# The first 300 pieces of a kernel that is written as a list of pieces, in another order

## The chip, the core and the metric

One Trainium2 chip, one core. The metric is device microseconds of one execution. The kernel before took 281.7, 282.6 and 284.32 us in three runs, median 282.6. One further execution was profiled. TensorE (PE) multiplies, VectorE (DVE), ScalarE (ACT) and GpSimd (POOL) work elementwise, SyncE (SP) issues the transfers. PE writes to PSUM, in four tiles here, called banks.

## The reference

Chunked attention feeds a gated causal convolution block. Batch 8, 8 heads, sequence 576, head width 64, model width 512.

```python
scores = scale * np.matmul(q_c, k_c.transpose(0, 1, 2, 4, 3))   # chunks of 64 tokens
scores = scores - np.max(scores, axis=-1, keepdims=True)
attn = np.exp(scores)
attn = attn / (np.sum(attn, axis=-1, keepdims=True) + 1e-09)
out = np.matmul(attn, v_c)                                      # becomes x, 8 x 576 x 512
...
gate_pre += conv_w[k][None, None, :] * xp[:, k:k + S, :]        # five taps
gate = 1.0 / (1.0 + np.exp(-gate_pre))
val = x @ w_val
return (gate * val @ w_out).astype(np.float32)
```

## The kernel before

The 4608 tokens are cut into nine groups of 512 (g = 0 to 8). In each group the eight heads stand as two pairs of tiles (p = 0, 1), and a pair can be worked on in two halves (b = 0, 1). The program is one list of short pieces, the string `ORDER` (line 19). The loop at line 634 runs through it and calls one small function for each piece. Every instruction goes through `run` (line 136, `tc.keep_in_program_order`), so each engine executes its own instructions in the order of the list, and all instructions carry line 137 in the profile. No scheduler changes it. Each engine is a queue of its own: a piece of PE that waits holds up every later piece of PE, and SP, POOL, DVE and ACT do likewise. SP keeps at most eight transfers in flight: each further one waits until the transfer eight places ahead of it has landed. `SLOTS` (line 85) gives each tile its buffer, each PSUM tile its bank, and each pair one of two probability tiles.

The pieces that matter here, with arguments group, pair, half:

- `lq`, `lk`, `lv`: load q, k, v of a pair, 512 KB, or 256 KB for a half. `lw n c`: load unit c of weight n (v for `w_val`, o for `w_out`), 512 KB. `lc`: load the convolution weights.
- `w1` to `w9`, `wa`, `wb`, `Q`, `wc`: the weights come as 64-bit floats and are made into a high and a low part of 32 bits (`v_hi`, `v_lo`). `Q` is three matmuls that sum parts on PE, with `wc` copying the sum out; `wa` and `wb` do that on POOL or DVE. `w5` is ACT, `w8` POOL, `w58` the two in one instruction on DVE. A D behind a name moves the piece to DVE, a G to POOL.
- `S`: scores, 16 small matmuls a half, which the trace shows as 32 rows. `mx`: maximum on DVE. `sb` then `ex`: subtract the maximum on DVE, exponential on ACT. In their place `mh`, `M`, `exM`: DVE splits the maximum into two parts (two instructions of 8 columns), PE subtracts them in the bank with four matmuls of 256 columns, ACT takes the exponential from the bank.
- `sm`: sum and reciprocal on DVE. `nm`: normalise on POOL. `T`: transposes on PE. `ec`: copy on ACT. `A`: probabilities times v on PE. `xr` (ACT) and `xd` (DVE): x as high and low part; `xc` keeps x for the convolution.
- `V g m c term`: one product of 512 columns for `val`. m is the output quarter, c the input quarter (c = 2 and 3 need pair 1, c = 0 and 1 pair 0), the term says which parts. Weight unit 3 holds c = 2, 3 with m = 2, 3; unit 2 c = 2, 3 with m = 0, 1; unit 1 c = 0, 1 with m = 2, 3; unit 0 the rest. `V 1 m c` without a term is three products.
- `k0`, `k`: taps of the convolution on ACT and DVE. `W n short`: matmuls on zeros that only keep PE active.

`HALVES` (line 632) makes pairs that have `xr` by halves keep their scores in a bank for each half, which holds for pair (0, 1). `LESS` (line 633) lists halves with an `M` piece; their score matmuls then accumulate. So a second `M` in the list is all that the program needs for the other half.

Of the kernel before, what the change touches and what calls it, by code (L numbers as in the profile page):

```python
# [22 lines left out]
T 0 1 0,ex 0 1 1,sb 0 0,ex 0 0,Q v 3,S 1 0 1,sm 0 1 1,sm 0 0,ec 0 1 0,wc v 3,wc v 2,S 1 0 0,lw v 0,w1G v 0,nm 0 1 1,w2 v 0,
mx 1 0,sb 1 0,T 0 1 1,ec 0 1 1,lv 0 1,A 0 1 0,xc 0 1 0,xr 0 1 0,xd 0 1 0,A 0 1 1,xr 0 1 1,xc 0 1 1,nm 0 0,T 0 0,ec 0 0,w3 v 0,
V 0 3 2 1,ex 1 0,V 0 2 2 2,V 0 1 3 1,w4 v 0,V 0 1 2 2,w9,V 0 1 2 1,w6 v 0,V 0 3 2 0,w7 v 0,w58 v 0,xd 0 1 1,lv 0 0,A 0 0,lw o 3,
V 0 1 2 0,V 0 2 3 1,V 0 0 2 2,w1G o 3,V 0 1 3 0,V 0 2 3 0,V 0 1 3 2,xr 0 0,V 0 2 3 2,xc 0 0,lw o 0,wa v 0,lk 1 1,V 0 0 2 1,
sm 1 0,lq 1 1,S 1 1 1,S 1 1 0,xd 0 0,V 0 0 0 0,nm 1 0,mx 1 1,wbD v 0,k0 0 2,V 0 3 3 2,k0 0 3,k0 0 1,ng 1 1,k 0 1 1,V 0 2 2 1,
V 0 3 1 1,w3 o 3,k0 0 0,k 0 0 1,T 1 0,V 0 0 3 2,V 0 2 0 2,w2 o 3,w4 o 3,V 0 1 1 1,V 0 2 1 2,lq 2 0,k 0 0 3,V 0 3 0 0,V 0 2 0 0,
ec 1 0,lv 1 0,w7 o 3,A 1 0,V 0 2 0 1,ea 1 1,k 0 2 1,V 0 3 1 2,k 0 3 2,w6 o 3,V 0 3 3 1,V 0 1 0 1,V 0 2 2 0,V 0 3 0 1,w58 o 3,
lv 1 1,k 0 0 2,V 0 2 1 1,V 0 3 3 0,rc 1 1,xr 1 0,xc 1 0,V 0 3 2 2,lk 2 0,V 0 0 1 0,V 0 0 1 2,V 0 3 1 0,V 0 2 1 0,V 0 3 0 2,  # L30
V 0 0 1 1,lw o 1,k 0 3 1,S 2 0 0,S 2 0 1,mx 2 0,vc 0 1,V 0 1 0 2,lq 2 1,w1G o 0,V 0 1 0 0,V 0 0 3 1,V 0 0 0 1,V 0 0 0 2,
V 0 1 1 0,lw o 2,lq 6 1,w5 o 0,xd 1 0,lq 8 1,lk 2 1,V 0 0 2 0,lk 3 0,lq 4 0,V 0 1 1 2,V 0 0 3 0,lv 3 1,nm 1 1,lq 3 1,lk 3 1,
lv 2 0,lk 4 0,vc 0 0,lq 3 0,w1G o 1,lv 2 1,w1G o 2,T 1 1,sb 2 0,V 1 2 0,ec 1 1,V 1 0 0,w3 o 1,k 0 2 2,ex 2 0,A 1 1,k 0 1 2,
w2 o 2,sm 2 0,S 2 1 0,xr 1 1,S 2 1 1,V 1 1 0,w5 o 2,xd 1 1,nm 2 0,w2 o 0,V 1 1 1,w2 o 1,V 1 0 1,mx 2 1,xc 1 1,V 1 3 2,ng 2 1,
k 0 3 3,V 1 0 3,ea 2 1,w3 o 2,V 1 0 2,k 0 0 4,V 1 1 2,k 0 1 3,T 2 0,w4 o 1,V 1 2 2,w7 o 1,k 0 2 3,V 1 3 3,k 0 1 4,V 1 3 0,
k 0 2 4,ec 2 0,V 1 3 1,w4 o 2,V 1 1 3,w3 o 0,k 0 3 4,S 3 0 0,sg 0 0,S 3 0 1,rc 2 1,w7 o 2,A 2 0,nm 2 1,mx 3 0,vc 1 0,V 1 2 3,
xr 2 0,sb 3 0,V 1 2 1,w8 o 2,sg 0 1,T 2 1,xd 2 0,vc 1 1,S 3 1 0,w4 o 0,S 3 1 1,ec 2 1,waD o 3,V 2 0 0,gs 0 0,xc 2 0,A 2 1,
w6 o 0,w7 o 0,V 2 2 0,gs 0 1,xr 2 1,V 2 0 1,lk 8 1,lq 5 1,w8 o 0,xd 2 1,V 2 1 0,V 2 2 1,ex 3 0,xcD 2 1,wa o 0,V 2 3 2,k0 1 0,
V 2 3 0,sm 3 0,wb o 0,gr 0 0,S 4 0 0,S 4 0 1,k0 1 2,mx 3 1,nm 3 0,V 2 2 2,gr 0 1,V 2 0 2,mx 4 0,k0 1 1,V 2 0 3,w6 o 2,hc 0 0,
ng 3 1,hc 1 0,sb 4 0,hc 0 1,V 2 2 3,wb o 3,ea 3 1,V 2 1 3,gdD 0 0,V 2 1 2,T 3 0,k 1 1 1,V 2 1 1,lv 4 0,lk 5 1,lk 7 0,lq 4 1,  # L40
lk 4 1,lv 3 0,lk 5 0,lv 8 0,waD o 2,V 2 3 1,wbD o 2,V 2 3 3,gdD 0 1,ec 3 0,S 4 1 0,S 4 1 1,rc 3 1,vc 2 0,k 1 1 2,A 3 0,ex 4 0,
nm 3 1,mx 4 1,P 0 2 0,w5 o 1,xcD 3 0,P 0 2 2,vc 2 1,P 0 3 2,w8 o 1,sb 4 1,w6 o 1,P 0 2 3,xr 3 0,T 3 1,wa o 1,sm 4 0,P 0 3 0,
ec 3 1,wb o 1,xd 3 0,S 5 1 0,ex 4 1,S 5 1 1,hc 2 1,A 3 1,nm 4 0,k0 3 0,sm 4 1,V 3 0 0,xr 3 1,P 0 3 3,mx 5 1,xc 3 1,nm 4 1,
P 0 2 1,k0 1 3,P 0 3 1,xd 3 1,k0 2 0,V 3 1 1,k0 2 2,k 1 0 1,V 3 0 1,oc 0 1,k 1 3 1,V 3 1 2,k 1 2 1,k0 3 1,T 4 0,k 1 1 3,V 3 2 0,
lv 4 1,ng 5 1,ec 4 0,k 1 0 2,V 3 2 3,k 1 3 2,k0 2 1,V 3 1 3,k 1 2 2,k0 2 3,V 3 3 0,k 1 3 3,ea 5 1,P 0 0 0,k 2 2 1,V 3 1 0,
k 2 0 1,V 3 3 3,k 1 2 3,V 3 2 2,k 2 2 2,V 3 0 2,k 1 1 4,P 0 1 0,k 1 0 3,P 0 1 3,k 1 2 4,k 1 0 4,P 0 0 1,k 2 3 1,P 0 1 1,sg 1 0,
k 1 3 4,V 3 0 3,lq 8 0,lk 6 0,lk 6 1,st 0 1,lq 7 0,lq 5 0,lk 8 0,lq 6 0,k 2 1 1,V 3 3 1,vc 3 0,k 2 3 2,P 0 0 3,sg 1 1,k 2 0 2,
T 4 1,gs 1 0,V 3 2 1,ec 4 1,V 3 3 2,rc 5 1,gr 1 0,gs 1 1,P 0 0 2,vc 3 1,A 4 0,gdD 1 0,gr 1 1,S 5 0 0,k 2 0 3,S 5 0 1,gd 1 1,
P 0 1 2,mx 5 0,P 1 2 0,oc 0 0,P 1 3 0,sb 5 0,xr 4 0,P 1 0 0,hc 2 0,k 2 3 3,xc 4 0,P 1 3 1,k 2 2 3,P 1 3 2,k 2 1 2,P 1 2 1,
k 2 3 4,P 1 3 3,ex 5 0,k 2 1 3,P 1 1 0,k 2 0 4,P 1 0 1,k 2 1 4,P 1 1 2,k 2 2 4,sg 2 0,P 1 0 2,xd 4 0,sg 2 1,P 1 2 3,gs 2 0,  # L50
# [16 lines left out]
k 3 2 2,V 6 0 2,gr 4 0,kk 6 1 3,V 7 0 0,gr 5 1,V 8 2 2,gdD 4 0,V 7 1 3,V 6 3 3,kk 6 2 3,V 6 1 1,k 5 1 2,V 8 3 0,k 5 0 2,V 7 1 0,
vc 8 1,kk 6 0 4,V 7 1 2,vc 6 0,V 6 2 3,k 3 1 3,gr 4 1,V 7 0 3,k 5 1 3,P 4 0 0,vc 6 1,k0D 8 2,P 4 0 1,k 5 0 3,gdD 4 1,P 4 2 0,
V 7 0 1,k 5 0 4,V 7 0 2,k 5 1 4,P 4 2 1,kk 6 1 4,sg 5 0,V 7 2 0,V 7 2 1,kk 6 3 1,sg 6 0,P 4 1 2,k0 8 3,k 3 1 4,P 4 3 1,kk 6 3 2,
V 7 2 2,P 4 0 3,gs 5 0,P 4 1 3,V 7 2 3,gdD 5 1,gr 5 0,V 7 3 0,sg 7 0,kk 6 3 3,P 4 2 3,P 4 0 2,gdD 5 0,V 7 1 1,P 4 1 1,gs 6 0,  # L70
# [630 lines left out]
```

## Time and profile before

| what | value |
|---|---|
| three runs | 281.7, 282.6, 284.32 us |
| the profiled execution, its own time | 284.87 us |
| its span, first to last instruction | 283.1 us |
| mean granted clock of PE | 0.994 |
| PE, DVE, ACT, POOL busy | 272.1, 240.2, 193.9, 61.7 us |

The profiled execution is 1.77 us longer than its span and 2.27 us longer than the median of the runs. In the page, a share of busy time is an average over the span. The chain of waits says what the end waited for, step by step; "issue" in it is time in which an engine waited for nothing that the profile shows. Queue q1 in the transfer view is data, queue q8 is named "instruction".

### The profile page before, as it was taken

What the parts mean: (1) busy time and instruction counts of PE and PEld (TensorE: products, weight loads), DVE (VectorE), ACT (ScalarE), POOL (GpSimd) and SP (SyncE); (2) the same over time, 40 slices, a digit from 0 to 9 for tenths busy, and PEclk for the clock granted to TensorE, in tenths of its full rate; (3) what the DMA queues carried; (4) which work ended last, traced back from release to release, by engine and by line L of the source; (5) the groups of instructions that cost most, each with busy time, mean ns of one, the idle gap of its engine ahead of it and who ended that gap; (6) DMA issues with size and microseconds to landing.
All of it is one profiled execution on the core that took longest, in us unless ns stands there. A gap on an engine that the chain in (4) does not pass through costs nothing.

```text
span 283.1 us, 7833 instructions
## 1 busy us (share of the span) xinstructions
PE 272.1 (96%) x3374; PEld 218.8 (77%) x3374; DVE 240.2 (85%) x301; ACT 193.9 (68%) x335; POOL 61.7 (22%) x62
## 2 busy tenths in 40 slices
...
GB/s 208 403 407 409 406 405 405 341 150 147 89 264 31 222 149 266 220 110 82 2 229 146 3 2 5 0 0 2 0 0 0 3 0 0 0 225 0 229 215 222
DMA packets 14754, 42.46 MB, mean 150 GB/s; under 512 B 1536, under 2 KB 1792, under 8 KB 14720
## 3 DMA queue, kind: packets, MB, share of 16 engines
...
q8 instruction: 26, 0.43, 0.6%
...
## 4 chain that ended last, share of the span: by engine, by line
PE 91%; DMA 5%; issue 1%; SPq 1%; POOL 1%; ACT 0%; POOLq 0%
PE b L137 91%; DMA z<-in_moe_w_val 3%; DMA z<-in_k 2%; SPq L137 1%; POOL z L137 1%; ACT z L137 0%; POOLq L137 0%
## 5 line engine op out<-in xcount | busy, mean ns | idle before, releaser
L137 PE MATMUL b<-z,v_hi 128*128 128x512 f32 x288 | 97.3, 404 | 0.0
L137 PE MATMUL b<-o_hi,z 128*128 128x512 f32 (+1 forms) x296 | 95.3, 393 | 0.0
L137 ACT COPY z<-b 128x1024 f32<-128x1024 f32 (+2 forms) x61 | 57.3, 967 | 41.1 <-PE b L137 41.0
L137 PEld LDWEIGHTS b<-o_hi,z 128*128 128x128 f32 x296 | 55.9, 190 | 12.9
L137 PEld LDWEIGHTS b<-z,v_hi 128*128 128x128 f32 x288 | 54.0, 188 | 13.0 <-DVE z L137 0.3
L137 PE MATMUL b<-o_lo,z 128*128 128x512 f32 (+1 forms) x148 | 57.9, 391 | 0.0
L137 PE MATMUL b<-z,v_lo 128*128 128x512 f32 x144 | 56.7, 398 | 0.0
L137 DVE SCALAR_TENSOR_TENSOR z<-z,cw,z 128x511 f32<-128x511 f32 (+3 forms) x72 | 51.0, 738 | 0.0
L137 POOL TENSOR_TENSOR z<-z,z 128x1024 fp32r<-128x1024 f32 (+2 forms) x8 | 16.1, 2021 | 116.5 <-ACT z L137 112.9
L137 POOL TENSOR_TENSOR z<-e_row,rs 128x1024 f32<-128x1024 f32 (+1 forms) x16 | 29.2, 1825 | 41.9 <-DVE rs L137 30.0
L137 PEld LDWEIGHTS b<-o_lo,z 128*128 128x128 f32 x148 | 28.1, 190 | 6.1
L137 ACT ACTIVATE z<-z 128x1024 f32<-128x1024 f32 (+3 forms) x24 | 20.3, 860 | 17.0 <-DVE z L137 16.9
L137 PEld LDWEIGHTS b<-z,v_lo 128*128 128x128 f32 x144 | 27.1, 188 | 5.4
L137 DVE SCALAR_TENSOR_TENSOR ys<-ys,cw 128x1022 f32<-128x1022 f32 (+3 forms) x24 | 30.1, 1273 | 0.0
L137 DVE TENSOR_TENSOR z<-z,z 128x1024 f32<-128x1024 f32 (+2 forms) x21 | 24.9, 1199 | 3.3 <-ACT z L137 3.2
L137 DVE TENSOR_TENSOR z<-b,z 128x1024 fp32r<-128x1024 f32 (+1 forms) x19 | 22.0, 1161 | 6.5 <-ACT z L137 5.8
L137 PEld LDWEIGHTS b<-z,z 64*64 64x64 f32 x1152 | 18.8, 135 | 9.5 <-issue 5.8
L137 PE MATMUL b<-z,z 64*64 64x64 f32 x1152 | 21.2, 221 | 4.9 <-issue 2.6
L137 DVE TENSOR_REDUCE mx<-b 128x16 f32<-128x1024 f32 (+1 forms) x19 | 21.5, 1142 | 1.8 <-PE b L137 1.7
L137 ACT CAST z<-b 128x1024 fp32r<-128x1024 f32 (+1 forms) x19 | 18.6, 989 | 5.2 <-PE b L137 5.0
L137 PE MATMUL b<-ident,z 128*128 128x128 f32 x144 | 19.2, 275 | 1.6 <-POOL z L137 1.6
L137 PEld LDWEIGHTS b<-ident,z 128*128 128x128 f32 x144 | 16.3, 140 | 4.2 <-POOL z L137 2.1
...
## 6 DMA issues: line engine op xcount, KB each, us to landing
...
z<-in_q SPq DMA_DIRECT2D x9, 512.0 KB, 10.2
...
```

The costliest lines, as they stand in the source:

```text
L137: return tc.keep_in_program_order(fn(*args, **kwargs))
```

## The change

The first 287 pieces are replaced by 288 pieces in another order; the remaining 744 stand as before. Within the 288, the second half of pair (0, 1) too has its maximum subtracted by PE: `mh 0 1 1`, `M 0 1 1`, `exM 0 1 1` in place of `sb 0 1 1` and `ex 0 1 1`. `w58 v 1` replaces `w5 v 1` and `w8D v 1`; `w5 o 3` and `w8 o 3` replace `w58 o 3`; `k0D 0 1` (DVE) replaces `k0 0 1` (ACT). The weight units of `w_val` are loaded as 1, 3, 2, 0 in place of 1, 2, 3, 0. The tables of buffers and banks follow the new order.

```diff
-ORDER = """zw,zr 0,lw v 1,zi,W 9 22,lc,w5 c 0,w1 c 0,w1 v 1,w3 v 1,w2D v 1,zr 1,w4 v 1,w7 v 1,w2 c 0,w3 c 0,w4 c 0,W 3,w5 v 1,lw v 2,
...
+ORDER = """zi,zs 0,zw,W 9 22,lw v 1,w1 v 1,w3 v 1,w2D v 1,w4 v 1,w6 v 1,w7 v 1,lw v 3,w1 v 3,lc,w5 c 0,lw v 2,w58 v 1,w2 v 3,w1 c 0,w2 c 0,
...
```

What moved, first on SP at the head of its queue. Before (v 1, convolution, v 2, q and k of the first half, v 3, then further halves):

```order
 L137 DMA z0_77<-in_moe_w_val 128x1024
 L137 DMA raw_cw_115<-in_moe_conv_w 128x40
 L137 DMA z3_138<-in_moe_w_val 128x1024
 L137 DMA z4_144<-in_q 128x512
 L137 DMA z5_149<-in_k 128x512
 L137 DMA z6_153<-in_moe_w_val 128x1024
```

The 13th to 16th transfers before (k and q of pair (1, 0), unit 0 of `w_val`, v of pair (0, 1)):

```order
 L137 DMA z10_275<-in_k 128x1024
 L137 DMA z11_277<-in_q 128x1024
 L137 DMA z12_335<-in_moe_w_val 128x1024
 L137 DMA z2_349<-in_v 128x1024
```

The change, the same places, 13th to 16th:

```order
 L137 DMA z10_284<-in_moe_w_val 128x1024
 L137 DMA z5_304<-in_q 128x1024
 L137 DMA z2_307<-in_k 128x1024
 L137 DMA z11_349<-in_v 128x1024
```

Unit 3 also went to the second place of the queue, so that q and k of the first half stand behind all of units 1, 3, 2. Unit 0 moved from the 15th place to the 13th, k of pair (1, 0) from the 13th to the 15th.

Second, PE from the scores of the first half to the normalised second half. Before (b3_220 are the scores of pair (0, 0), b1_280 the transposes of pair (0, 1), b3_292 the scores of pair (1, 0)):

```order
 L137 MATMUL b0_155<-mr1_187,signed_63 128x256 x4
 L137 MATMUL b3_220<-z8_190,z9_210 64x64 x32
 L137 MATMUL b2_261<-z0_140,ident_62 128x512
 L137 MATMUL b2_261<-v_hi_67,signed_63 128x512
 L137 MATMUL b2_261<-z4_237,signed_63 128x512
 L137 MATMUL b1_280<-ident_62,z8_268 128x128 x4
 L137 MATMUL b0_288<-z7_173,ident_62 128x512
 L137 MATMUL b0_288<-v_hi_67,signed_63 128x512
 L137 MATMUL b0_288<-z9_272,signed_63 128x512
 L137 MATMUL b3_292<-z10_275,z11_277 64x64 x32
 L137 MATMUL b1_280<-ident_62,z8_268 128x128 x4
```

The change (b1_187 is the second half of pair (0, 1), b2_228 the scores of pair (0, 0)):

```order
 L137 MATMUL b0_166<-mr1_207,signed_63 128x256 x4
 L137 MATMUL b2_228<-z9_226,z8_220 64x64 x32
 L137 MATMUL b1_187<-mr2_222,signed_63 128x256 x4
 L137 MATMUL b0_279<-z1_155,ident_62 128x512
 L137 MATMUL b0_279<-v_hi_67,signed_63 128x512
 L137 MATMUL b0_279<-z6_217,signed_63 128x512
 L137 MATMUL b1_287<-z3_124,ident_62 128x512
 L137 MATMUL b1_287<-v_hi_67,signed_63 128x512
 L137 MATMUL b1_287<-z0_151,signed_63 128x512
 L137 MATMUL b2_294<-ident_62,z6_291 128x128 x4
 L137 MATMUL b3_309<-z2_307,z5_304 64x64 x32
```

Four matmuls were added, and both weight sums now stand ahead of the first transposes.

Third, POOL, whose queue feeds the transposes. Before (z4_237 and z9_272 are `w8`, z8_268 and z9_393 are `nm`, z4_337 is `w1G v 0`):

```order
 L137 TENSOR_TENSOR z4_237<-z4_237,z0_140 128x512
 L137 TENSOR_TENSOR z8_268<-e_row0_65,rs1_265 128x2x256
 L137 TENSOR_TENSOR z9_272<-z9_272,z7_173 128x512
 L137 TENSOR_SCALAR z4_337<-z12_335 128x512
 L137 TENSOR_TENSOR z8_268<-e_row0_65,rs2_309 128x2x256
```

The change:

```order
 L137 TENSOR_TENSOR z6_217<-z6_217,z1_155 128x512
 L137 TENSOR_TENSOR z0_151<-z0_151,z3_124 128x512
 L137 TENSOR_TENSOR z6_291<-e_row0_65,rs1_246 128x2x256
 L137 TENSOR_SCALAR z0_300<-z10_284 128x512
 L137 TENSOR_TENSOR z6_291<-e_row0_65,rs2_276 128x2x256
```

The piece that reads unit 0 still stands ahead of the second `nm`; what it reads is now the 13th transfer.

## Rows read from the trace of the kernel before

**Rows 1.** Page: busy time and share of each engine; chain that ended last.

```profile
PE 272.1 (96%) x3374; PEld 218.8 (77%) x3374; DVE 240.2 (85%) x301; ACT 193.9 (68%) x335; POOL 61.7 (22%) x62
...
PE 91%; DMA 5%; issue 1%; SPq 1%; POOL 1%; ACT 0%; POOLq 0%
```

**Rows 2.** Timeline of PE to 31 us: start, duration, instruction, [idle before <-releaser].

```profile
8.33 0.69 PE L137 MATMUL b<-z,z 64*64 64x64 f32 x32 [1.49 <-DMA z<-in_k]
...
11.95 0.80 PE L137 MATMUL b<-mr,signed 128*128 128x256 f32 x4 [0.30 <-DVE mr L137]
...
18.26 1.16 PE L137 MATMUL b<-z,z 64*64 64x64 f32 x64
20.53 0.66 PE L137 MATMUL b<-ident,z 128*128 128x128 f32 x4 [1.11 <-POOL z L137]
21.11 1.44 PE L137 MATMUL b<-z,z 64*64 64x64 f32 x64
22.48 1.09 PE L137 MATMUL b<-ident,z 128*128 128x128 f32 x8
23.33 0.48 PE L137 MATMUL b<-z,v_lo 128*128 128x512 f32 x1
...
26.80 1.33 PE L137 MATMUL b<-z,v_hi 128*128 128x512 f32 x5
...
30.43 1.27 PE L137 MATMUL b<-ident,z 128*128 128x128 f32 x8
```

**Rows 3.** Timeline of POOL, 14 to 22 us.

```profile
14.03 1.27 POOL L137 TENSOR_TENSOR z<-z,z 128x512 fp32r<-128x512 f32 x1 [12.60 <-ACT z L137]
15.26 1.05 POOL L137 TENSOR_TENSOR z<-e_row,rs 128x512 f32<-128x512 f32 x1
...
18.79 0.67 POOL L137 TENSOR_SCALAR z<-z 128x512 f32<-128x512 f32 x1 [1.25 <-DMA z<-in_moe_w_val]
19.42 2.92 POOL L137 TENSOR_TENSOR z<-e_row,rs 128x512 f32<-128x512 f32 x2
```

**Rows 4.** Timeline of SP: issues; x2 is two issues.

```profile
9.50 0.33 SPq L137 DMA_DIRECT2D z<-in_q  x1
...
18.65 1.61 SPq L137 DMA_DIRECT2D z<-in_v  x2
```

**Rows 5.** Timeline of DVE, 11 to 20 us.

```profile
11.93 0.17 DVE L137 TENSOR_TENSOR mr<-mx,mr 128x8 fp32r<-128x8 f32 x1
...
13.07 0.69 DVE L137 TENSOR_TENSOR e_row<-b,mx 128x512 f32<-128x512 f32 x1
...
17.58 0.20 DVE L137 RECIPROCAL rs<-rs 128x8 f32<-128x8 f32 x1
...
19.41 0.25 DVE L137 RECIPROCAL rs<-rs 128x16 f32<-128x16 f32 x1
```

**Rows 6.** Chain of waits in order of time: start, us, what.

```profile
31.03 0.01 issue
...
84.04 2.62 issue
```

**Rows 7.** Page: the instruction queue over the span (packets, MB, share).

```profile
q8 instruction: 26, 0.43, 0.6%
```

**Rows 8.** Transfer view, 15.8 to 48 us.

```profile
q8 instruction: 6, 0.10, 1.3%
```

**Rows 9.** Transfer view, 28.6 to 29.7 us.

```profile
q8 instruction: 1, 0.02, 5.8%
```

**Rows 10.** Transfer view, 84.2 to 85.3 us.

```profile
q8 instruction: 1, 0.02, 5.4%
```

**Rows 11.** Windows: length, busy (instructions) of PE, PEld, DVE, ACT, POOL, clock, DMA, GB/s.

```profile
0.00:31.04 31.04, 25.65 (x473) 16.82 (x473) 24.49 (x47) 21.07 (x36) 12.39 (x18) 1.00 0.93 361
...
0.00:84.10 84.10, 78.66 (x1485) 60.18 (x1486) 75.04 (x118) 72.47 (x176) 36.62 (x38) 1.00 0.80 302
```

**Rows 12.** Windows, 87 to 91 us, after the idle time at 84 us.

```profile
87.00:91.00 4.00, 4.00 (x11) 3.17 (x12) 2.02 (x3) 3.77 (x5) 0.00 (x0) 0.57 0.00 0
```

More of the change, by code (lines that the diff above doesn't have):

```diff
@@ L23 @@
[L23 to L50, printed above, removed]
@@ L67 @@
[L67 to L70, printed above, removed]
@@ new lines @@
+w3 c 0,w4 c 0,lk 0 1 0,lq 0 1 0,zs 1,w7 c 0,Q v 1,w5 v 3,wc v 1,w3 v 3,w1 v 2,w4 v 3,w2 v 2,w3 v 2,w8D c 0,w7 v 3,W 3,S 0 1 0,
+mx 0 1 0,lk 0 1 1,lq 0 1 1,S 0 1 1,zr 1,w4 v 2,w6 v 2,mh 0 1 0,mx 0 1 1,M 0 1 0,exM 0 1 0,w5 v 2,w7 v 2,lq 0 0 1,mh 0 1 1,w9,
+lk 0 0 1,S 0 0 1,zr 0,sm 0 1 0,lq 0 0 0,lk 0 0 0,S 0 0 0,mx 0 0,w8 v 2,sb 0 0,M 0 1 1,exM 0 1 1,sm 0 1 1,Q v 2,w6 v 3,lw v 0,
+w8 v 3,Q v 3,nm 0 1 0,ex 0 0,T 0 1 0,wc v 2,w1G v 0,w2 v 0,nm 0 1 1,lq 1 0,wc v 3,lk 1 0,S 1 0 0,S 1 0 1,T 0 1 1,sm 0 0,lv 0 1,
@@ new lines @@
+ec 0 1 0,A 0 1 0,nm 0 0,mx 1 0,sb 1 0,ec 0 1 1,xr 0 1 0,xc 0 1 0,A 0 1 1,T 0 0,xr 0 1 1,V 0 3 3 0,V 0 2 3 1,xd 0 1 0,xc 0 1 1,
+ec 0 0,V 0 2 2 2,w3 v 0,w4 v 0,ex 1 0,V 0 1 3 0,w7 v 0,lv 0 0,w58 v 0,w6 v 0,wa v 0,V 0 0 2 1,V 0 3 2 2,A 0 0,xr 0 0,V 0 3 2 0,
+sm 1 0,V 0 2 2 1,V 0 1 2 2,xc 0 0,xd 0 1 1,V 0 2 3 0,xd 0 0,V 0 1 2 0,nm 1 0,V 0 0 3 1,k0 0 3,lw o 2,V 0 2 0 0,V 0 3 1 1,lk 1 1,
+lq 1 1,S 1 1 0,S 1 1 1,V 0 0 2 2,k0 0 0,mx 1 1,V 0 3 3 2,T 1 0,w5 o 2,V 0 2 0 1,V 0 3 3 1,lw o 3,V 0 3 0 1,V 0 3 1 2,lq 2 0,
@@ new lines @@
+w1G o 3,w3 o 3,V 0 0 0 0,V 0 2 2 0,ng 1 1,V 0 2 1 1,lw o 0,V 0 1 3 2,lv 1 0,V 0 0 1 2,w2 o 3,V 0 0 1 0,w4 o 3,V 0 1 0 0,ec 1 0,
+V 0 1 1 0,A 1 0,V 0 2 1 0,V 0 2 3 2,ea 1 1,xr 1 0,k 0 0 2,w3 o 0,V 0 1 0 2,V 0 0 3 2,k0D 0 1,V 0 1 2 1,k 0 0 4,V 0 3 1 0,xc 1 0,
+lw o 1,V 0 0 3 0,wbD v 0,w3 o 2,k 0 1 4,V 0 3 0 0,lv 3 1,V 0 1 1 2,w7 o 3,lk 2 0,S 2 0 1,S 2 0 0,w5 o 0,k 0 3 2,V 0 0 0 2,
+V 0 2 1 2,V 0 3 0 2,w3 o 1,rc 1 1,V 0 2 0 2,V 0 3 2 1,lv 1 1,k 0 0 1,V 0 0 1 1,V 0 0 2 0,xd 1 0,k0 0 2,lq 2 1,mx 2 0,vc 0 1,
@@ new lines @@
+lk 2 1,sb 2 0,w5 o 3,nm 1 1,k 0 2 3,w1G o 1,V 0 1 3 1,T 1 1,ec 1 1,V 0 1 1 1,V 0 1 0 1,S 2 1 0,k 0 1 3,ex 2 0,S 2 1 1,w1G o 2,
+w2 o 1,A 1 1,xr 1 1,V 0 0 0 1,sm 2 0,xd 1 1,V 1 1 0,mx 2 1,w2 o 2,ng 2 1,V 1 0 0,k 0 2 2,vc 0 0,V 1 1 1,w4 o 1,k 0 2 4,w6 o 3,
+V 1 0 1,w4 o 2,k 0 3 3,k 0 2 1,V 1 1 3,V 1 3 3,V 1 0 3,V 1 1 2,w7 o 1,xc 1 1,k 0 3 1,w7 o 2,V 1 2 2,lk 3 0,ea 2 1,rc 2 1,
+k 0 1 1,V 1 0 2,w8 o 3,w1G o 0,V 1 3 0,k 0 3 4,lk 4 0,k 0 1 2,w2 o 0,nm 2 0,T 2 0,lq 4 0,V 1 3 1,lq 3 0,S 3 0 0,lq 3 1,S 3 0 1,
@@ new lines @@
+ec 2 0,lv 2 0,k 0 0 3,vc 1 0,A 2 0,lq 8 1,mx 3 0,V 1 2 0,nm 2 1,V 1 3 2,sg 0 0,lv 2 1,lk 3 1,lq 6 1,V 1 2 3,xr 2 0,sb 3 0,
+V 1 2 1,w8 o 2,sg 0 1,T 2 1,xd 2 0,vc 1 1,S 3 1 0,w4 o 0,S 3 1 1,ec 2 1,waD o 3,V 2 0 0,gs 0 0,xc 2 0,A 2 1,w6 o 0,w7 o 0,
+V 2 2 0,gs 0 1,xr 2 1,V 2 0 1,lk 8 1,lq 5 1,w8 o 0,xd 2 1,V 2 1 0,V 2 2 1,ex 3 0,xcD 2 1,wa o 0,V 2 3 2,k0 1 0,V 2 3 0,sm 3 0,
+wb o 0,gr 0 0,S 4 0 0,S 4 0 1,k0 1 2,mx 3 1,nm 3 0,V 2 2 2,gr 0 1,V 2 0 2,mx 4 0,k0 1 1,V 2 0 3,w6 o 2,hc 0 0,ng 3 1,hc 1 0,
```

83 lines of the change are left out of this document (48 added, 35 removed), and 12 rows, old and new, of the table z.

## The prediction

> **What bounds the kernel now.** I read the page first. PE is busy 96% of the span and is 91% of the chain that ended last [rows 1]; the other engines are busy less. Then the counts by stretch [rows 11]: between 31.04 and 84.10 us PE is busy 78.66 - 25.65 = 53.01 of 53.06 us. So the kernel is a start, in which PE waits, and then a dense stream, and whatever starts the stream earlier by x ends the kernel earlier by x, as long as nothing later holds the stream up. The timeline of PE [rows 2] shows the start: PE waits 1.49 us for the first k, 0.30 for a split maximum, 1.11 for POOL at the second half's transposes, and its first product of `val` starts at 23.33. From there I looked for what could hold up the stream. The chain of waits has one long item, 2.62 us of "issue" up to 86.66 us, beginning at 84.04 [rows 6], and a tiny one of the same kind, 0.01 us, at 31.03. "Issue" names no other engine, so I looked at the transfers: just ahead of both stands a packet of the queue named instruction, one in 28.6 to 29.7 us and one in 84.2 to 85.3 [rows 9, 10]. The counts fit: 473 + 473 matmuls and weight loads up to 31.04 us and 1485 + 1486 up to 84.10 [rows 11], a difference of 2025. The whole trace has 2 x 3374 = 6748 of them [rows 1] and 26 packets [rows 7], 260 a packet, so the two places lie 7.8, that is about eight packets apart. I read both as places where PE reaches the end of a block of its instructions: at 84 us the next block came late, at 31.03 it came just in time.
>
> **The change part by part.**
>
> *Transfers.* SP's 512 KB transfers follow each other by 1.61 - 0.33 = 1.28 us [rows 4]. Unit 3 now stands ahead of the first q and k, so these land where the sixth transfer did: SP's 14th issue, which waits for that landing, is at 9.50 [rows 4]. The first scores start at about 9.5 instead of 8.33 and end at 9.5 + 0.69 = 10.2 [rows 2]. The second half's k and q keep their 7th and 8th place. The matmuls that wait for the maximum started at 11.95 [rows 2], so 1.75 us are left for a maximum and its split. Cost between nothing and 1.2 us; I take nothing, since rows 2 show PE waiting only 0.30 us there, for DVE. Without that cover it would be 1.2.
>
> *Subtraction on PE.* It removes 0.69 us of DVE and adds two instructions of 0.17 [rows 5]. On PE it adds four matmuls, 0.80 us [rows 2]. They stand behind the scores of pair (0, 0), in a stretch in which PE waits, and nothing behind them on PE is ready before POOL: they cost nothing. DVE still does the maximum and subtraction of pair (0, 0) ahead of the second half's sum, so I leave that sum's end at 17.58 + 0.20 = 17.78 [rows 5].
>
> *POOL.* Before, `w1G v 0` waited 1.25 us for unit 0 and started at 18.79, and behind it stood the second half's normalisation, at 19.42 [rows 3]. Now unit 0 is two transfers, 2.56 us, earlier and POOL does not wait for it. POOL's queue is then 14.03 + 2 x 1.27 + 1.05 + 0.67 = 18.3, later than DVE's 17.78; the normalisation ends at 18.3 + 1.1 = 19.4 (1.1 is 20.53 - 19.42). What is late next is k of pair (1, 0), which takes the place that unit 0 had and lands at 18.65 [rows 4]. Its scores stand ahead on PE and take 1.16 [rows 2], to 19.8. The transposes start there instead of 20.53, 0.7 us earlier. v of pair (0, 1) stays 16th and lands at 18.65 + 1.28 = 19.93, before it is needed. Then A takes 1.44 [rows 2], the next normalisation starts when DVE's reciprocal ends, 19.41 + 0.25 = 19.66 [rows 5], takes 1.8 of the 2.92 [rows 3] and ends at 21.5: both give a first product at about 22.6 instead of 23.33, **0.7 us earlier**. Bounds: 0, if k of pair (1, 0) or DVE is later than I say, and 1.1, all of PE's wait for POOL.
>
> *Edits with one answer.* `w58 v 1`, `w5 o 3`, `w8 o 3`, `k0D 0 1` move work of 0.4 to 1.3 us between ACT, DVE and POOL. None is PE's; POOL has the room at 22% busy [rows 1]. If DVE is the one that PE waits for, the difference is one instruction of 0.69. The order of the 18 products ahead of T of group 1 costs nothing by itself: each is (1.33 - 0.40) / 4 = 0.23 us in any order (0.40 is the duration of one such matmul).
>
> *Instruction blocks.* PE's list has eight more instructions (four matmuls with their weight loads) ahead of T of group 1, and now 16 products stand ahead of it instead of 18, four instructions fewer. So the block's end falls two transposes earlier. With the lead of 0.7 and two products less PE reaches T at 30.43 - 0.7 - 2 x 0.23 = 29.3 us. But the packets come evenly: six from 15.8 to 48 us [rows 8], 32.2 / 5 = 6.4 us from one to the next if the stretch holds five spacings, at a time when data keep the DMA engines busy (0.93 up to 31.04 us [rows 11]), and the third at 28.6 [rows 9]. In both places PE went on 2.4 us after the packet's start (31.04 - 28.6 and 86.66 - 84.2). If the packet comes at the same time, PE idles from about 29.5 to 31.03, and then stands two transposes, 2 x (1.27 - 0.28) / 7 = 0.28 us, and two products, 0.46 us, **behind** the kernel before, 0.74 us (0.28 is what the last one's modelled end overlaps). If the packet comes with PE's need, the lead of 0.7 stays. No row shows how the time of a packet is set, so this is the unknown term, from -0.7 to +0.74 us. I take **+0.3**: nearer to the late end because the evenly spaced packets and the 0.01 us speak for it, less than it because ACT and DVE run ahead while PE idles, which may save short waits of PE later.
>
> On this term the Trainium skill, page "Runtime: NRT & Kernel Launch", section "Instruction fetch mechanics", speaks for the lead: blocks of 16 KiB are fetched while the one before runs, and the cost of crossing is mostly hidden. By it the sum would be 284.87 - 0.7 = 284.2 us for the profiled execution, the first rival's time. The 2.62 us at 84 us [rows 6] disagree with it at that one place.
>
> **Sum.** 284.87 + 0.3 = 285.2 us for the profiled execution, which is 2.27 above the median; against the median, 282.6 + 0.3 = **282.9 us**. What this kernel's measurement can tell from no change is about 1%, 2.8 us; my forecast is within it.
>
> **Rivals.**
> 1. *The lead goes through.* The packet comes when PE needs it: 282.6 - 0.7 = 281.9 us. For it: PE waits 0.01 us at 31.03, not more. Against: the even spacing. Chance 0.30.
> 2. *The stop at 84 us disappears.* The list is shifted by eight instructions, and if the late packet is asked for ahead of the data that delayed it, PE gains 2.62 us [rows 6] and the time at half clock behind it: from 87 to 91 us the mean granted clock was 0.57 [rows 12], that is 1.2 GHz for most of it, 0.43 x 4 = 1.7 us lost. 282.6 - 4.3 = 278.3. Against: the pieces around it and their order of transfers are the same. Chance 0.10.
> 3. *Slower: one more late packet.* A block's end now falls in the denser starts, and a packet misses its place: the price is that of the stop at 84 us, 4.3 us, up to a whole spacing of 6.4. 282.6 + 4.3 = 286.9. It decides as soon as PE has used up a block, some 130 matmuls, before the next packet is there; 64 small matmuls take only 1.16 us. Chance 0.10.
> 4. *It doesn't do what it says.* The list would have to keep its order through the recording layer; PE has four more matmuls of 256 columns, so this is excluded.
>
> **How the numbers follow.** Forecast 0.50, rivals 0.30, 0.10, 0.10. The forecast's own range is 281.9 to 283.5, and with 0.8 us for the spread of the runs' median 281.1 to 284.3. Rivals 2 and 3 together are 0.2, so the range ends between them and the forecast: 280.3 to 285.2. Faster by over 1% means rival 2 and a little of 1: 0.14. Slower by over 1%: rival 3 and a little of the forecast: 0.14. Within 1%: 0.72.
>
> **What would show it.** In the changed profile: the first product at 22.6 us; PE's row for the second half's transposes without 1.1 us behind POOL; POOL's `w1G v 0` without a wait for a transfer; the first scores at 9.5. For the forecast, 1 to 1.5 us of "issue" before 31.1 us, with an instruction packet in 28.6 to 29.7; for rival 1, none. The stop of 2.6 us near 84 us should stand, with its half clock. I am wrong if the first product starts later than 23.3, or if "issue" in the chain adds up to far more or less than 2.62 + 1.5 us.

## The result and the profile after

| | before | after |
|---|---|---|
| median of 20 executions each | 283.05 us (281.7 to 285.7) | 285.52 us (284.16 to 288.67) |
| ratio, with 95% interval | | 1.0085 (1.0062 to 1.0108) |
| the profiled execution, its span | 284.87, 283.1 us | 285.41, 283.6 us |
| mean granted clock in it | 0.994 | 1.000 |

The kernel became slower: by 2.47 us in the medians, by 0.85% in the ratio. Ratios, here and below, leave out executions in a slower state (of after one, 288.67 us) and can differ from the quotient of the two medians, by 0.35% at most. The forecast was 282.9 with a range up to 285.2, so the time lies 0.3 us above the range. The forecast's change was +0.3 us, a little slower; the measured one is eight times that. Part of the distance in us is the yardstick: the three runs known then had the median 282.6, the twenty here have 283.05.

The two profiled executions differ by only 0.54 us, and this must be understood first: that of before is one of its longer ones, with a stop of 2.62 us and 3.4 us at half clock behind it [rows 6, 12]; that of after kept the full clock there.

The page after, in answer to [rows 1]: busy times.

```profile
PE 271.4 (96%) x3378; PEld 218.0 (77%) x3378; DVE 242.7 (86%) x302; ACT 193.5 (68%) x334; POOL 64.1 (23%) x63
```

PE has its four matmuls more, and DVE is busier by 2.5 us although a little work was taken from it. The chain of after in order of time (start, us, what), in answer to [rows 6]:

```profile
30.24 0.92 issue
...
43.97 0.09 issue
...
60.88 2.86 ACT z L137 x3
...
87.21 1.40 issue
```

So PE stops at three places behind its start: in T 1 0, which [rows 6] had at 0.01 us; ahead of V 2 0 0 at 63.78 us, where before had nothing and where ACT now stands in the chain; and at 87.21, where before had 2.62.

The timeline of PE after to 32 us, in answer to [rows 2]:

```profile
9.53 0.69 PE L137 MATMUL b<-z,z 64*64 64x64 f32 x32
...
18.42 1.16 PE L137 MATMUL b<-z,z 64*64 64x64 f32 x64 [0.39 <-DMA z<-in_k]
19.51 0.65 PE L137 MATMUL b<-ident,z 128*128 128x128 f32 x4
20.90 1.18 PE L137 MATMUL b<-z,z 64*64 64x64 f32 x64 [0.73 <-ACT z L137]
...
23.33 0.50 PE L137 MATMUL b<-z,v_hi 128*128 128x512 f32 x1 [0.23 <-ACT z L137]
...
29.75 0.49 PE L137 MATMUL b<-ident,z 128*128 128x128 f32 x3
31.16 0.77 PE L137 MATMUL b<-ident,z 128*128 128x128 f32 x5 [0.92 <-issue]
```

The first scores are at 9.53 (forecast 9.5) and the second half's transposes at 19.51 (forecast 19.8). But then PE waits for ACT, and the first product is at 23.33, exactly as before. T 1 0 is cut in two: three transposes, the stop, five transposes. What ACT did at that place, and what POOL did (in answer to [rows 3]):

```profile
20.26 1.07 ACT L137 COPY z<-b 128x512 f32<-128x512 f32 x2 [1.11 <-PE b L137]
```

```profile
17.97 1.06 POOL L137 TENSOR_TENSOR z<-e_row,rs 128x512 f32<-128x512 f32 x1
```

POOL's `w1G v 0` (17.34, 0.67 us) has no wait any more, and the second half's normalisation starts at 17.97 instead of 19.42. But ACT stands idle until 20.26 and then copies both halves one after the other (ec 0 1 0, ec 0 1 1): in the new list ec 0 1 0 stands behind T 0 1 1, which writes the same bank, so the first copy too waits for the second transposes.

The new stop is at S 3 1. PE, DVE and POOL of after from 54 to 64 us (the row with x4 is four taps: k 0 1 1, k 0 3 4, k 0 1 2, k 0 0 3; behind them mx 3 0 and sb 3 0; POOL's two are nm 2 1 and w8 o 2):

```profile
59.53 1.03 PE L137 MATMUL b<-ident,z 128*128 128x128 f32 x8
62.45 1.25 PE L137 MATMUL b<-ys 64*64 64x64 f32 x64 [1.88 <-issue]
63.78 0.50 PE L137 MATMUL b<-z,v_hi 128*128 128x512 f32 x1
```

```profile
54.39 0.25 DVE L137 RECIPROCAL rs<-rs 128x16 f32<-128x16 f32 x1
54.56 5.32 DVE L137 SCALAR_TENSOR_TENSOR z<-z,cw,z 128x511 f32<-128x511 f32 x4
59.80 1.21 DVE L137 TENSOR_REDUCE mx<-b 128x16 f32<-128x1024 f32 x1
61.12 1.23 DVE L137 TENSOR_TENSOR e_row<-b,mx 128x1024 f32<-128x1024 f32 x1
```

```profile
54.81 2.17 POOL L137 TENSOR_TENSOR z<-e_row,rs 128x1024 f32<-128x1024 f32 x1 [5.99 <-DVE rs L137]
56.94 1.73 POOL L137 TENSOR_TENSOR z<-z,z 128x512 f32<-128x512 f32 x1
```

The second and the third of the four taps by themselves (timeline of DVE, 55.25 to 57.3 and 57.6 to 59 us):

```profile
55.14 2.39 DVE L137 SCALAR_TENSOR_TENSOR z<-z,cw,z 128x508 f32<-128x508 f32 x1
```

```profile
57.45 1.77 DVE L137 SCALAR_TENSOR_TENSOR z<-z,cw,z 128x510 f32<-128x510 f32 x1
```

The same place before, PE, DVE and then POOL:

```profile
58.50 1.03 PE L137 MATMUL b<-ident,z 128*128 128x128 f32 x8
59.47 1.16 PE L137 MATMUL b<-z,z 64*64 64x64 f32 x64
60.56 0.50 PE L137 MATMUL b<-z,v_hi 128*128 128x512 f32 x1
```

```profile
54.55 0.74 DVE L137 SCALAR_TENSOR_TENSOR z<-z,cw,z 128x508 f32<-128x508 f32 x1
...
56.20 1.23 DVE L137 TENSOR_REDUCE mx<-b 128x16 f32<-128x1024 f32 x1 [0.25 <-PE b L137]
57.46 1.22 DVE L137 TENSOR_TENSOR e_row<-b,mx 128x1024 f32<-128x1024 f32 x1
```

```profile
55.84 1.91 POOL L137 TENSOR_TENSOR z<-e_row,rs 128x1024 f32<-128x1024 f32 x1 [7.93 <-DVE rs L137]
57.70 1.29 POOL L137 TENSOR_TENSOR z<-z,z 128x512 f32<-128x512 f32 x1
```

Before, all taps of group 0 were done when POOL began, and beside POOL DVE did mx 3 0 and sb 3 0, which read a bank. After, four taps stand there and take 5.32 us, where four undisturbed ones take some 2.7 (2.73 in g1 below). PE's wait ahead of 62.45 is called "issue", but it is one for DVE: S 3 1 writes the bank that sb 3 0 reads, and sb 3 0 had ended only 0.1 us before, at 61.12 + 1.23 = 62.35. All 72 taps of the program after (busy us, mean ns; before they were busy 51.0 us, 738 ns each):

```profile
L137 DVE SCALAR_TENSOR_TENSOR z<-z,cw,z 128x511 f32<-128x511 f32 (+3 forms) x72 | 54.4, 785 | 0.0
```

Of the 3.4 us more, 2.6 are these four (5.32 against 2.73); the rest are two taps from 43.09 us on, which take 2.16 us together, also beside POOL. mx 3 0 is 3.60 later (59.80 against 56.20): 2.6 of it is the taps' delay beside POOL, the other 1.0 DVE's new order.

The account, by the start of the same instruction before and after: the transposes T 2 1 58.50 and 59.53, +1.03; S 3 1 59.47 and 62.45, +2.98; the first product V 2 0 0 60.56 and 63.78, +3.22; PE's resumption in A 3 1 86.66 [rows 6] and 88.60, +1.94, since the stop is 1.40 instead of 2.62; the last copy on ACT 280.16 and 280.69, +0.53, since before ran at half clock for a while behind its stop, which cost it 1.94 - 0.53 = 1.41 us. As an estimate from these rows, an execution of before without that half clock would take 284.87 - 1.41 = 283.5 us, near its median, and end about 2 us ahead of after. The stop in A 3 1 comes at the same count of instructions in both: up to it PE did 1485 matmuls and 1486 weight loads, as in [rows 11].

```profile
0.00:87.21 87.21, 79.36 (x1485) 60.61 (x1486) 77.34 (x119) 72.11 (x175) 38.93 (x39) 1.00 0.77 291
```

Ahead of both stops stands an instruction packet, from 28.6 to 29.7 us, where [rows 9] had it, and, in answer to [rows 10], in the transfer view of 86.3 to 87.4 us:

```profile
q8 instruction: 1, 0.02, 5.0%
```

### The profile page after: what moved, and what is told of

The parts are those of the page before. It is cut to its first block, busy times and chain, and to the rows that moved or that the text cites. A ratio compares the mean times of both kernels' runs of the same rounds, so it can differ in the third digit from the quotient of the medians.

```text
span 283.6 us, 7838 instructions
## 1 busy us (share of the span) xinstructions
PE 271.4 (96%) x3378; PEld 218.0 (77%) x3378; DVE 242.7 (86%) x302; ACT 193.5 (68%) x334; POOL 64.1 (23%) x63
## 4 chain that ended last, share of the span: by engine, by line
PE 90%; DMA 4%; ACT 2%; issue 1%; DVE 1%; ACTq 0%
PE b L137 90%; DMA z<-in_k 3%; ACT z L137 2%; DMA z<-in_moe_w_val 1%; DVE z L137 1%; ACT signed L137 0%; ACT v_lo L137 0%; DVE cw_t L137 0%; ACTq L137 0%; ACT cw_t L137 0%
## 5 line engine op out<-in xcount | busy, mean ns | idle before, releaser
L137 ACT COPY z<-b 128x1024 f32<-128x1024 f32 (+2 forms) x63 | 59.3, 965 | 40.5 <-PE b L137 39.9
L137 PEld LDWEIGHTS b<-o_hi,z 128*128 128x128 f32 x296 | 55.1, 188 | 12.8
L137 DVE SCALAR_TENSOR_TENSOR z<-z,cw,z 128x511 f32<-128x511 f32 (+3 forms) x72 | 54.4, 785 | 0.0
L137 POOL TENSOR_TENSOR z<-z,z 128x512 f32<-128x512 f32 (+2 forms) x9 | 16.7, 1864 | 97.9 <-ACT z L137 79.4
L137 DVE TENSOR_TENSOR z<-z,z 128x1024 f32<-128x1024 f32 (+1 forms) x19 | 23.0, 1227 | 2.5 <-ACT z L137 2.5
```

The costliest lines, as they stand in the source:

```text
L137: return tc.keep_in_program_order(fn(*args, **kwargs))
```

## The experiments

They ran in four sets; a ratio is to the executions of the kernel before in the same set (medians 282.39 to 283.13 us). Diffs show the pieces of the list; the tables of buffers keep each tile in its place. The lists are a line or two longer there, so all instructions carry line 138 or 139 in place of 137.

**Is DVE's lateness at S 3 1 the loss? e1: two taps behind sb 3 0.**

```diff
 k 0 3 4,lk 4 0,
-k 0 1 2,
...
-k 0 0 3,
...
-sg 0 0,
...
 sb 3 0,
+k 0 1 2,k 0 0 3,sg 0 0,
```

> The changed kernel with two taps (k 0 1 2 and k 0 0 3) moved behind sb 3 0 on DVE, and the sigmoid that needs them behind them. Theory A: PE's 1.85 us wait at S 3 1 (60.56 to 62.41) is DVE's: it stood in two taps, 2.39 and 1.77 us instead of 0.74, beside work of POOL, and reached mx 3 0 only at 59.80. Then mx 3 0 starts near 57.5, sb 3 0 ends near 60.1, S 3 1 starts without a wait at about 60.6, and the time falls by 1.9 to 2.3 us, to 283.1 to 283.6. Rival B: the stream is held there by the transfers that the wait also names, or gives the gain back at the next stop for instructions (1.40 us at 87.2 in the changed kernel, 2.62 at 84.0 in the kernel before): 284.5 to 285.5.

Measured: 286.39 us, ratio 1.0105 (1.0056 to 1.0154). S 3 1 starts at 59.92 without a wait, but no time is gained: PE waits 2.64 us at V 2 0 0. Its chain names a second way from the taps to PE:

```profile
63.72 0.50 PE L139 MATMUL b<-z,v_hi 128*128 128x512 f32 x1 [2.64 <-ACT z L139]
```

```profile
54.06 2.88 DVE z L139 x2
...
59.33 1.41 DVE z L139 x2
...
61.72 1.95 ACT z L139 x2
```

Taps, then the sigmoids on ACT that need them, then vc 1 1, which stands behind the sigmoids and frees the bank for V 2 0 0. Theory A was half the truth; rival B named the wrong place. In the changed kernel PE reached V 2 0 0 less than 0.1 us before vc 1 1 was done, so taking away the wait at S 3 1 alone gains nothing.

**f1: the sigmoids out of the way as well.**

```diff
-k 0 1 2,
...
-k 0 0 3,
...
-sg 0 0,
...
 sb 3 0,
+k 0 1 2,k 0 0 3,
...
-sg 0 1,
...
 ec 2 1,
+sg 0 0,sg 0 1,
```

> The changed kernel with k 0 1 2 and k 0 0 3 behind sb 3 0 on DVE, as in e1, and both sigmoids of group 0 (sg 0 0, sg 0 1) behind the copy ec 2 1 on ACT. Theory A: DVE's lateness reaches PE in two ways, by sb 3 0 (S 3 1 waited to 62.41) and by the sigmoids, which wait for the taps and hold up vc 1 1 and ec 2 1 on ACT (in e1 the first product of V 2 0 0 waited to 63.71 for vc 1 1). With both out of the way neither wait stands, V 2 0 0 starts near 61.5 instead of 63.78, and the time falls by about 2.2 us against the changed kernel, to a ratio of 1.000 to 1.002 to the kernel before. Rival B: the gain is lost again at the next stop for instructions (84 to 88 us), which grows from 1.4 to 2.6 us or more: ratio 1.005 and more.

Measured: 285.75 us, ratio 1.0109 (1.0075 to 1.0143). V 2 0 0 starts at 61.30, as expected, and the lost time comes back one piece later:

```profile
65.65 0.50 PE L139 MATMUL b<-z,v_hi 128*128 128x512 f32 x1 [1.89 <-ACT z L139]
```

```profile
61.40 1.28 ACT L139 ACT_TABLE_LOAD   x1
```

The sigmoids run from 62.69 for 2.00 us, with a table load ahead of them that ACT's idle time had covered. They now hold up xc 2 0, and V 2 2 0 needs the bank that xc 2 0 reads. Pushing late work aside only moves the wait; the time lost on DVE has to be won back on DVE.

**Are the taps long because of POOL? e3: w8 o 2 on DVE instead.**

```diff
-w8 o 2,
+w8D o 2,
```

> The changed kernel with w8 o 2 on DVE (behind sb 3 0) instead of POOL. Theory A: a tap takes long exactly while POOL multiplies a tile; without POOL's w8 o 2 (56.94, 1.73 us) the tap k 0 1 2 takes 0.74 us again instead of 1.77, while k 0 3 4, beside POOL's nm 2 1, stays at 2.39. mx 3 0 starts 1.0 us earlier, the wait at S 3 1 falls from 1.85 to about 0.8 us, and the time falls by 0.8 to 1.1 us, to about 284.4. Rival B: the taps are long for another reason (the transfers that land then): both stay long and the time stays at 285.4, or grows by the 0.7 us more on DVE.

Measured: 284.5 us, ratio 1.0079 (1.0045 to 1.0112), which cannot tell 1 us from nothing. The rows can: the four taps take 4.29 us, 1.03 less, and PE's wait at S 3 1 is 0.86 us. V 2 0 0 starts at 62.55, 1.23 earlier, and the stop in A 3 1 takes 0.5 of that back (1.92 us for 1.40).

```profile
54.36 4.29 DVE L139 SCALAR_TENSOR_TENSOR z<-z,cw,z 128x511 f32<-128x511 f32 x4
```

**f2: the other way round, the kernel before with two taps moved beside POOL.**

```diff
-k 0 2 4,
...
-k 0 3 4,
...
 w7 o 2,
+k 0 2 4,k 0 3 4,
```

> The kernel before with two taps (k 0 2 4 and k 0 3 4) moved four and six places back on DVE, behind w7 o 2, so that they run while POOL multiplies (nm 2 1, w8 o 2). The same instructions, no other edit. Theory A: a tap, which reads two tiles of SBUF, waits until POOL's instruction ends; the two take about 2.3 and 1.3 us instead of 0.74 each, mx 3 0 starts at about 58.1 instead of 56.20, and PE waits about 1.1 us at S 3 1 (59.47). Time: 0.5 to 1.1 us more, unless the later stop of 2.62 us takes some of it back. Rival B: the taps were long in the changed kernel for another reason (their place in the transfers' traffic, a late ACT): they stay at 0.74, and the time stays.

Measured: 284.71 us, ratio 1.0064 (1.0029 to 1.0099). DVE, POOL and PE:

```profile
55.34 4.12 DVE L138 SCALAR_TENSOR_TENSOR z<-z,cw,z 128x508 f32<-128x508 f32 x2
```

```profile
55.32 1.90 POOL L138 TENSOR_TENSOR z<-e_row,rs 128x1024 f32<-128x1024 f32 x1 [6.63 <-DVE rs L138]
57.18 1.74 POOL L138 TENSOR_TENSOR z<-z,z 128x512 f32<-128x512 f32 x1
```

```profile
61.96 1.16 PE L138 MATMUL b<-z,z 64*64 64x64 f32 x64 [1.63 <-issue]
```

The same instructions, two of them a few places later: 4.12 us for what takes 1.4 alone, a new wait of 1.63 us at S 3 1, and the kernel before is slower by three quarters of what the change cost. The wait is the part that the rows give to the taps; this execution was 0.79 us behind already in T 1 0, ahead of the moved taps (31.83 against 31.04).

**g1: one piece moved, so that no tap runs beside POOL.** nm 2 1 needs rc 2 1; with rc 2 1 behind the taps POOL starts when they are done.

```diff
-rc 2 1,
 k 0 1 1,
...
 k 0 0 3,
+rc 2 1,
```

> The changed kernel with one piece moved: rc 2 1 (the reciprocal that lets POOL start nm 2 1) stands behind the four taps k 0 1 1, k 0 3 4, k 0 1 2, k 0 0 3 instead of ahead of them. Theory A: then no tap runs beside POOL; each takes 0.66 to 0.74 us, nm 2 1 starts near 57.4, mx 3 0 near 57.3, and POOL's two multiplications run beside mx 3 0 and sb 3 0, which read PSUM and are not held up. sg 0 0 starts near 57, vc 1 1 is in time, S 3 1 and V 2 0 0 do not wait; T 2 1 may wait 0.1 to 0.4 us for nm 2 1. V 2 0 0 starts near 61.8 instead of 63.78, and the time falls by 1.7 to 2.2 us, to a ratio of 1.001 to 1.003. Rival B (as in f1): a later wait takes the gain back, or nm 2 1 comes so late that T 2 1 holds PE instead: ratio 1.006 or more.

Measured: 282.75 us, ratio 0.9995 (0.9959 to 1.0031). DVE, POOL, PE:

```profile
53.81 2.73 DVE L139 SCALAR_TENSOR_TENSOR z<-z,cw,z 128x511 f32<-128x511 f32 x4
```

```profile
57.08 1.91 POOL L139 TENSOR_TENSOR z<-e_row,rs 128x1024 f32<-128x1024 f32 x1 [8.62 <-DVE rs L139]
58.95 1.30 POOL L139 TENSOR_TENSOR z<-z,z 128x512 f32<-128x512 f32 x1
```

```profile
60.12 1.16 PE L139 MATMUL b<-ys 64*64 64x64 f32 x64
```

Four taps in 2.73 instead of 5.32 us, POOL back at 1.91 and 1.30, no wait at either place (V 2 0 0 starts at 61.22), and the whole loss is gone, though the stop in T 1 0 stands (0.93 in its chain). By rows V 2 0 0 starts 2.56 us ahead of the changed kernel; 0.37 of that stood already at T 1 0 (30.79 against 31.16), so the moved piece is worth 2.19, which is what S 3 1 and V 2 0 0 had cost. The rest is luck: the stop in A 3 1 is 0.81 us here, 1.40 after.

**The stop in T 1 0. f4: the subtraction on DVE again (eight instructions of PE less); f3: 40 instructions of PE less at the start.**

```diff
-mh 0 1 1,
+sb 0 1 1,
...
-M 0 1 1,exM 0 1 1,
+ex 0 1 1,
```

> The changed kernel with the second half's maximum subtracted on DVE again (sb 0 1 1, ex 0 1 1 in place of mh 0 1 1, M 0 1 1, exM 0 1 1); PE's list loses 8 instructions there. Theory A: the subtraction on PE cost nothing where it stands; the first product stays at 23.3 within 0.3 us; the stop inside T 1 0 ends at the same time, 31.2, but eight instructions later in the list, so at most 0.6 us is gained: time 0 to 0.6 us less than the changed kernel. Rival B: the four matmuls or the exponential from the bank are what makes the start late: the first product comes 0.5 us or more earlier and the time falls by 1 us or more.

Measured: 284.36 us, ratio 1.0057 (1.003 to 1.0084); first product at 23.43. T 1 0:

```profile
29.83 0.93 PE L139 MATMUL b<-ident,z 128*128 128x128 f32 x7
31.04 0.33 PE L139 MATMUL b<-ident,z 128*128 128x128 f32 x1 [0.28 <-issue]
```

Eight instructions less ahead, and the cut lies exactly four transposes (eight instructions) further on. PE reaches it at 30.76 instead of 30.24 and goes on at 31.04 instead of 31.16: the end of the stop does not follow PE.

```diff
-W 9 22,
+W 9 2,
```

> The changed kernel with 20 of the 22 short matmuls on zeros at the start left out (W 9 2), which takes 40 instructions off PE's list ahead of everything else. Theory A: the stop inside T 1 0 (0.92 us before 31.16) is the end of a block of 256 instructions whose successor comes at 28.6; with 40 fewer ahead, the block ends 40 instructions later, behind T 1 0, where PE comes after 31.1, so the stop is gone, PE is about 0.9 us earlier from there to 60 us, and the time falls by 0 to 0.9 us (S 3 1 waits for DVE, which may eat it). Rival B: the stop in T 1 0 belongs to something else than the place in the list, and stays.

Measured: 282.98 us, ratio 1.0044 (1.0009 to 1.008). T 1 0 is not cut any more, and neither is A 3 1; the wait at S 3 1 stays, 1.6 us.

```profile
29.54 1.04 PE L139 MATMUL b<-ident,z 128*128 128x128 f32 x8
```

**Does a lead at the start reach the end? e2: the first copy early.**

```diff
 T 0 1 0,
+ec 0 1 0,
...
-ec 0 1 0,
```

> The changed kernel with the copy ec 0 1 0 right behind T 0 1 0, as in the kernel before, instead of behind T 0 1 1. Theory A: the lead that was forecast for the first product went because ACT copies both halves only after T 0 1 1 (copies at 20.26 and 20.74, PE waits 0.73 us for them); now the first product starts at 22.6 to 22.9 instead of 23.33. But the instruction packet near 28.6 sets when T 1 0 goes on, 31.1 to 31.2, so the stop inside T 1 0 grows from 0.92 to about 1.4 us and the time stays within 0.3 us of 285.4. Rival B: the packet comes as much earlier as PE does, the stop stays at 0.9 and the time falls by 0.5 to 0.7 us.

Measured: 286.17 us, ratio 1.0118 (1.007 to 1.0166). PE waits for no copy any more; its first product is at 23.04, 0.3 earlier although k of pair (1, 0) landed 0.5 later in this execution. T 1 0 is cut at the same transpose and goes on at 31.36. But the lead was gone before it got there: A 0 0 took 1.61 us (from 24.63) instead of 1.16, and PE reached the cut at 30.38, after at 30.24. So the stop did not grow to 1.4 us, and this run cannot tell the theories apart.

```profile
31.36 0.77 PE L139 MATMUL b<-ident,z 128*128 128x128 f32 x5 [0.98 <-issue]
```

**The stop in A 3 1. e4: four transfers of that time later; g3: the kernel before with 52 instructions less.**

```diff
-lv 4 1,
...
-lq 8 0,lk 6 0,lk 6 1,st 0 1,
+st 0 1,lv 4 1,lq 8 0,lk 6 0,lk 6 1,
```

> The changed kernel with four transfers (lv 4 1, lq 8 0, lk 6 0, lk 6 1), issued from 79.88 to 86.45, moved behind the first output (93.8). Theory A: the stop inside A 3 1 (1.40 us idle, 1.7 lost, at 87.2) is an instruction packet that was wanted from about 80.5 and came at 86.37 behind these transfers; without them it comes within 2 us, PE does not stop, and the time falls by 1.4 to 1.7 us, to about 283.8, and no run shows the lower mean clock. Rival B: the packet's time does not depend on these transfers: stop and time stay, 285.4, or the late v and k make PE wait at S 6 0 or A 4 1 near 123 us.

Measured: 283.78 us, ratio 1.0045 (1.0021 to 1.007). A 3 1 runs through, and in the transfer view of 81 to 87 us the instruction packet is the only one.

```profile
87.23 1.32 PE L139 MATMUL b<-z,z 64*64 64x64 f32 x64
```

Theory A, but for one point: the lower mean clock was still there in the profiled execution (0.994). From 63.26 to 66.67 us, behind the wait at S 3 1, which this edit leaves, the granted clock was half, and PE lost 1.4 us: V 2 0 0 starts 0.4 ahead of the changed kernel and the place of the stop is reached 1.0 behind it. That lateness alone would have shortened the stop. The packet's own time speaks for the transfers: it follows the packet before it by 5.2 us (80.6 and 85.8), after by 6.8 (79.6 and 86.4). So do the executions with a mean clock of 0.999 and more: 283.44 to 284.12 us here (10 of 12), 284.16 to 285.78 after (10 of 20).

```diff
-W 9 22,
+W 3 2,
```

> The kernel before with W 3 2 in place of W 9 22 (26 matmuls on zeros, 52 instructions less ahead of everything). Theory A: the end of the block that stopped PE for 2.62 us inside A 3 1 at 84.04 now falls some 12 products behind A 3 1, at 87 us, when its instructions are there: no stop, no half clock, and the time falls by 2.5 us, to a ratio of 0.991. Rival B: the stop belongs to the transfers of that time and comes at another place of the list, or the first scores run at the lower clock because PE was less busy ahead of them: 0.996 to 1.002.

Measured: 286.07 us, ratio 1.0097 (1.006 to 1.0134). Rival B, and twice over. A 3 1 runs through, but another block now ends between dense matmuls of 47 us, and PE waits there; and from 8 to 14 us, after 4.92 us without work, the granted clock was 0.50, 1.2 GHz.

```profile
46.91 3.51 issue
```

```profile
8.00:14.00 6.00, 4.87 (x68) 3.10 (x68) 4.88 (x13) 2.18 (x5) 0.00 (x0) 0.50 1.05 399
```

**A faster kernel. g2 is g1 with f3's edit, h1 is g1 with two long matmuls more there.**

```diff
-W 9 22,
+W 9 2,
...
-rc 2 1,
 k 0 1 1,
...
 k 0 0 3,
+rc 2 1,
```

> g1 and, as in f3, 20 of the short matmuls on zeros left out at the start. Theory A: the two repairs add up, since they mend different stops (T 1 0 and A 3 1 by the list, S 3 1 and V 2 0 0 by the taps): f3 stood at 1.0044, so the ratio is 0.996 to 0.999, faster than the kernel before. Rival B: with PE earlier by 0.9 us from T 1 0 on, DVE and ACT are the ones that set the time until 62 us, and the sum is no better than g1 or f3 alone, 1.002 to 1.004.

Measured: 281.41 us, ratio 0.9979 (0.9939 to 1.002). No stop at any of the three places, but the granted clock was 0.57 from 8 to 12 us.

```diff
-W 9 22,
+W 11 2,
```

> g2 with W 11 2 in place of W 9 2: two long matmuls on zeros more, so that they end near 5.7 us as in the changed kernel, while PE's list is still 36 instructions shorter. Theory A: in g2 the clock fell to 0.50 from 9 to 12 us in most executions because the matmuls on zeros ended half a microsecond sooner; with the longer ones it stays at 1.00 there, T 1 0 and A 3 1 still have no stop, and the ratio is 0.993 to 0.997, faster than both kernels. Rival B: the low clock at the start belongs to the work itself and stays in most executions: 0.997 to 0.999, as g2.

Measured: 280.84 us, ratio 0.9931 (0.989 to 0.9971), faster than both kernels. The granted clock is 1.00 from 8 to 14 us, and the time is in the expected range, but theory A's reason does not hold: the matmuls on zeros ended at 5.22 us, not near 5.7, and no later than in g2 (5.31). Against g2 the intervals overlap. From 30 to 87 us PE is busy 56.41 of 57.00:

```profile
30.00:87.00 57.00, 56.41 (x1034) 46.18 (x1032) 54.20 (x76) 54.86 (x146) 28.39 (x23) 1.00 0.71 264
```

## Why the prediction failed

- **Transfers: right.** The first scores are at 9.53 (forecast 9.5), the waits behind them are small, the cost is nothing.
- **Subtraction on PE: right.** Undone in f4, the first product stays (23.43). The price that the rows show is eight instructions in PE's list, which put the cut in T 1 0 four transposes earlier.
- **POOL: half right.** The wait is gone and the transposes start at 19.51 (forecast 19.8). The 0.7 us behind them did not come: I followed POOL and DVE to the first product, not ACT's place in the list. ec 0 1 0 stood behind T 0 1 1, a row of the order I had not looked at. Instead of -0.7 the term was 0. Whether a lead would have passed T 1 0 no run shows: in e2 it was gone before. f4, where PE came to the cut half a us later than after and went on 0.12 earlier, speaks against it.
- **Instruction blocks: mechanism right, size short.** Taken +0.3, late end +0.74, measured 0.92 of stop and +1.03 at T 2 1, that is the late end and with it 0.12 (PE went on at 31.16 instead of 31.04), 0.09 at 43.97 and 0.08 in small parts. The packet of 28.6 us was where it had been, and the cut fell as counted. I took less than the late end in the hope that DVE and ACT run ahead in PE's idle time, for which I had no row. The Trainium skill, page "Runtime: NRT & Kernel Launch", section "Instruction fetch mechanics", has the crossing mostly hidden. The trace of after disagrees at two places, with 0.92 and 1.40 us; in f3, where the ends fall elsewhere, the longest stop of this kind is 0.31 us, at 43.20.
- **"Edits with one answer" is the step that failed.** I read "none is PE's" and "whatever starts the stream earlier ends the kernel earlier, as long as nothing later holds the stream up" off a count that showed a dense PE from 31 to 84 us. That density came from the old order and was no property of the stretch: DVE, 85% busy, reached mx 3 0 with 0.25 us of waiting for PE, that is, just in time. I priced the reordered 31 to 60 us at nothing without asking what each DVE instruction now runs beside. The price was 2.6 us of taps beside POOL and a DVE later by 3.60 us at mx 3 0, of which 1.88 us reached PE as a wait at S 3 1 and 0.2 more at V 2 0 0. Of the rivals, the third had the sign (286.9), but with another cause, a packet; that is no hit.
- **The stop at 84 us stood**, in the same block, with 1.40 us for 2.62. PE came to it 3.17 us later (87.21 against 84.04), the packet only 2.1 us later (86.3 against 84.2 [rows 10]). So it gave back some of what the two other places took, which is luck: no term of the prediction had it.

By rows, then: +1.03 (T 1 0 and 43.97), +2.2 (S 3 1 and V 2 0 0), -1.3 (A 3 1), 1.9 us; the medians say 2.47. The remaining 0.5 us was not traced; it is of the size of the spread of the start from one execution to the next (with the same list up to there, T 1 0 went on at 31.16 us after and at 30.79 in g1).

Of the prediction's own signs the first product stands at 23.33, just over the 23.3 that would make it wrong, and the two stops called "issue" are 0.92 and 1.40 us, where it named 1 to 1.5 and 2.6. One slip in its sums changed nothing: the late end gives 282.6 + 0.74 = 283.3, not 283.5, as the upper end of the forecast's own range.
